# A two-pass channel-attention kernel: smaller last loads in pass one, and another order of the first stores in pass two

## The chip, the cores and the metric

The kernel runs on one core of a Trainium2 chip. The metric is the device time of one execution in microseconds (us). Three runs of the kernel before took 722.88, 720.63 and 720.82 us, so the median is 720.82 us.

## The reference

`x` has 384 x 384 pixels of 384 bf16 channels, 113 MB. Each channel is averaged over all pixels, the average is multiplied by one weight, goes through a sigmoid, and the result scales that channel everywhere:

```python
def reference(x, w1d):
    B, H, W, C = x.shape
    k = 1
    pad = k // 2
    g = jnp.einsum("bhwc->bc", x) / (H * W)
    gp = jnp.pad(g, ((0, 0), (pad, pad)))
    s = jnp.zeros_like(g)
    for i in range(k):
        s = s + gp[:, i:i + C] * w1d[i]
    s = _sigmoid(s)
    return x * s[:, None, None, :]
```

No output element can be written before the last input element has been read.

## The kernel before, in words

**Rows.** The 147,456 pixels lie on 128 partitions, so each partition owns 1152 pixels. A "row" below is one pixel on all 128 partitions: 128 x 384 bf16, 98,304 bytes in HBM and 768 bytes on each partition. The one big buffer, `arena`, holds 275 rows and cannot hold all 1152. So 367 rows are *kept* from pass one to pass two, and 785 rows are *streamed*: read in pass one for the sum alone and read again in pass two. In all 1152 + 785 rows are loaded and 1152 are stored, 3089 row transfers.

**Keeping more than fits.** Most kept rows are *folded* (`fold`, L292): four rows go into the space of three by moving the exponent bits of the fourth row (`u`) into bits of the other three that are the same for all plausible values. VectorE does this with bit operations (L276, L282), and ScalarE tests that no value was out of line (L313). Folding uses two scratch areas of eight rows, `T` (rows 259 to 266 of `arena`) and `Y` (rows 267 to 274). In pass two `unfold` (L470) takes the rows apart again and scales them. It writes into eight rows beside each group and uses `Y` as scratch. 71 kept rows are *raw*, not folded: `U` and `V` (8 rows each, beside the two columns of folded groups), the 39 rows of `A` (three slots of 13: `S1`, `S2`, `S3`), and at the very end the scratch areas themselves, `T` and `Y`, which lie next to each other and are filled once the last fold is done.

**Pass one.** Every load is issued from the SP queue (L236) and every row is summed over the partitions by a TensorE matmul against a matrix of ones, into one PSUM bank (L242). `take_raw` (L438) loads the raw rows and sums them. The loop at L437 does this, in program order, for `S2`, `U`, `S3`, `S1`, `V`, `Y`, and for `T` in two loads of 5 and 3 rows. Then ScalarE computes the sigmoid `s_bf` (L443) and puts a copy of it into PSUM (L447).

**Pass two** has a hand-written planner (L564 to L759), a Python loop that runs while the kernel is built. It keeps a model clock `now` that advances in steps of 0.05 us, and it decides in which order instructions are put on the queues. The names that matter here:

- `landed` is the queue of pieces in `arena` that wait to be scaled by VectorE (`scale`, L456). The loop at L620 fills it first, with `Y`, `U`, `T` and `V`. L622 adds the slots `S1` and `S2`. Three pieces of `S3` (4, 4 and 5 rows) are scaled by GpSimd instead, beside VectorE (`alongside`, L628).
- When a piece is scaled, `send` and then `store` (L466) put its store on the SP queue. In the planner's model a store occupies the DMA for `n * ROW + PER_STORE` us, with `ROW` 0.2267 and `PER_STORE` 0.061. It begins at the earliest `LAT` = 2 us after its issue, one transfer after the other, and is known to be over `SEEN` = 1.5 us after its end.
- `stored` (L609) then marks its rows `idle`, that is, free for a load. Rows of `Y`, `U` and `V` are not marked. They are what the unfolding of the two columns needs (`needed`, L607), and a column's first group starts only when its rows are stored.
- The load rule (L739 to L749) takes the longest run of idle rows. It issues a load of streamed rows if the run has at least 32 rows, or has 8 and the planned backlog of the DMA (`ahead`) is below `LOW` = 9 us, or if `ahead` is below `LAST` = 4 us.
- VectorE takes a landed piece if there is one, else the next step of an unfolding (L695 to L707).

**Queues.** All big transfers go through the one SP queue, in program order. A load into rows whose store is still under way makes SP wait until that store has landed, and everything behind it on SP waits too (L112, L118). Each SP transfer takes one of 24 semaphore lanes in turn, and also waits for the transfer 24 places before it (L46 to L52).

Of the kernel before, what the change touches and what calls it, by code (L numbers as in the profile page):

```python
# [127 lines left out]
def kernel(  # L128
# [28 lines left out]
    U = 3 * PIECE + PAIRS * 3 * PAIR  # L157
    G0 = U + PAIR
    V = G0 + PAIRS * 3 * PAIR
    A = V + PAIR  # L160
    N_A = 39
    T = A + N_A
    Y = T + 2 * PIECE
# [60 lines left out]
    def raw(a):  # L224

        return c_raw + (a - U if a < G0 else PAIR + a - V)
# [167 lines left out]
    S1, S2, S3 = ([slot] for slot in SLOTS)  # L394
# [38 lines left out]
    def take_raw(a, n):  # L433
        load(KEPT, a, raw(a), raw(a) + n)
        sum_rows(a, n)

    for a, n in S2 + [(U, 8)] + S3 + S1 + [(V, 8), (Y, 8), (T, 5), (T + 5, 3)]:  # L437
        take_raw(a, n)  # L438
    assert summed[0] == RPP

# [176 lines left out]
        return f  # L617


    for a, n, end in ((Y, 4, True), (Y + 4, 4, True), (U, 4, True), (U + 4, 4, True), (T, 8, True), (V, 8, True)):  # L620
        landed.append((KEPT, a, raw(a), n, end))
    for a, n in SLOTS[:2]:  # L622
        landed.append((KEPT, a, raw(a), n, True))
# [64 lines left out]
    while True:  # L688

        if dve_at <= now:  # L690
# [4 lines left out]
            if landed and (ahead < PENDING or not can):  # L695
                chunk, a, lo, n, end = landed.popleft()
# [13 lines left out]
        if alongside and alongside[0][0] <= now:  # L710
            _, chunk, a, lo, n = alongside.popleft()
            store(chunk, a, lo, lo + n)
            moves.append([now + LAT, n * ROW + PER_STORE, stored(a, n)])
        while waiting and waiting[0][0] <= now:
            _, n, then, chunk, a, lo, known = waiting.popleft()
# [12 lines left out]
        if bank_at is None and len(line) <= total - BANKS_AT and got and max(got)[0] >= PS * 4 // 3:  # L728
            a = max(got)[1]
# [9 lines left out]
        if got and todo < N_STREAM:  # L739
            n, a = max(got)  # L740
            n = min(n, CAP, N_STREAM - todo)
# [52 lines left out]
```

## Time and profile before

| what | us |
|---|---|
| median of the three runs | 720.82 |
| span of the profiled execution (first to last instruction) | 719.4 |
| first big load issued | 0.96 |
| sigmoid begins (L443) | 268.13 |
| first scale of pass two (L456) begins | 268.74 |
| first store issued on SP | 269.73 |
| first load of pass two issued on SP | 278.69 |
| VectorE busy in all | 493.9 |
| TensorE busy in all | 213.0 |

The profile gives no execution time of its own for the profiled execution beyond its span. The span of 719.4 us is 1.4 us below the median of the runs. An "issue" row on SP is the short time in which the sequencer hands a transfer over (0.33 us for most). The time "to landing" runs from that issue to the last of the transfer's 16 completion counts.

### The profile page before, as it was taken

To read this page: it belongs to the slowest core of one execution; us is meant where nothing else is said; L and a number is where in the kernel's file an instruction comes from. 1 tells how busy PE (TensorE), PEld (TensorE's weight loads), DVE (VectorE), ACT (ScalarE), POOL (GpSimd) and SP (SyncE) were. 2 spreads that over 40 slices of the span, in tenths; PEclk is the share of its full clock that TensorE was granted. 3 is DMA by queue.
4 is the path that set the end of the run, shared out by engine and by line. 5 is a ranking of instruction groups with operands and counts; after the bars stand their busy time and mean duration, and the time that the engine had idled before them with its cause. 6 is when DMAs were issued, how large, how long until landed. Compare 5 with 4: busy or idle time off the path is not lost.

```text
span 719.4 us, 2061 instructions
## 1 busy us (share of the span) xinstructions
PE 213.0 (30%) x1202; PEld 0.3 (0%) x3; DVE 493.9 (69%) x471; ACT 115.7 (16%) x93; POOL 10.6 (1%) x7
## 2 busy tenths in 40 slices
PE   4677788897987770000000000000000000000000
PEld 0000000000000000000000000000000000000000
DVE  4600004788999719988999998999998985095500
ACT  3600003566677610002000000000000000000000
POOL 0000000000000005000000000000000000000000
PEclk9899999999999995555555555555555555555555
DMA  9999999999999979999999999999999999999997
GB/s 379 435 433 435 426 428 435 438 434 425 426 426 429 427 326 376 421 391 423 430 430 437 430 428 441 428 433 435 430 436 433 429 437 428 441 432 427 440 439 314
DMA packets 20174, 303.79 MB, mean 422 GB/s; under 512 B 2243, under 2 KB 2243, under 8 KB 6083
## 3 DMA queue, kind: packets, MB, share of 16 engines
q1 hardware_dynamic: 20160, 303.67, 99.0%
q8 instruction: 4, 0.07, 0.0%
q14 instruction: 8, 0.06, 0.0%
q10 hardware_dynamic: 2, 0.00, 0.0%
HBM read 190.41 MB, written 113.25 MB: 422 GB/s over the span
## 4 chain that ended last, share of the span: by engine, by line
DMA 63%; DVE 23%; PE 6%; ACT 2%; another core or an unknown queue 1%; SPq 1%; issue 0%; DVEq 0%
DMA arena<-in_x_dram 42%; DMA out_dram<-arena 20%; DVE arena L456 16%; PE bank L242 6%; DVE arena L276 4%; DVE arena L282 3%; ACT arena L313 2%; SPq L236 1%; ACT s_bf L443 0%; SPq L789 0%; DVEq L112 0%; SPq L106 0%
## 5 line engine op out<-in xcount | busy, mean ns | idle before, releaser
L456 DVE TENSOR_TENSOR arena<-arena,s_bf 128x4608 bf16<-128x4608 bf16 (+8 forms) x97 | 228.7, 2390 | 68.2 <-DMA arena<-in_x_dram 52.2
L276 DVE TENSOR_SCALAR arena<-arena 128x1536 uint16<-128x1536 uint16 (+2 forms) x247 | 145.3, 633 | 111.6 <-DMA arena<-in_x_dram 101.8
L242 PE MATMUL bank<-arena,ones 128*128 128x384 bf16 x1151 | 204.6, 339 | 46.3 <-DMA arena<-in_x_dram 46.3
L313 ACT ACTIVATE arena<-arena 128x3072 uint16<-128x3072 uint16 (+1 forms) x38 | 102.4, 2696 | 142.1 <-DVE arena L276 142.1
L282 DVE TENSOR_TENSOR arena<-arena 128x1536 uint16<-128x1536 uint16 (+2 forms) x114 | 121.0, 1061 | 5.2 <-PE bank L242 2.8
L529 PE MATMUL bank<-odd,ones 128*128 128x1 bf16 x1 | 0.2, 187 | 322.6 <-DVE odd L524 322.6
L456 POOL TENSOR_TENSOR arena<-arena,s_bf 128x1536 bf16<-128x1536 bf16 (+1 forms) x3 | 10.4, 3481 | 268.7 <-ACT bank L447 268.7
L386 ACT COPY arena<-bank 128x512 uint32<-128x512 uint32 (+1 forms) x7 | 4.0, 570 | 58.2 <-DMA out_dram<-arena 58.1
L456 DVE TENSOR_TENSOR arena<-arena,bank 128x1536 bf16<-128x1536 bf16 (+2 forms) x7 | 11.3, 1689 | 0.0
L242 PE MATMUL bank<-zeros,ones 128*128 128x384 bf16 x48 | 8.3, 326 | 0.0
L313 ACT ACTIVATION_READ_ACCUMULATOR arena<-arena 128x1 f32 x38 | 7.1, 186 | 0.0
L386 ACT COPY bank<-arena 128x512 uint32<-128x512 uint32 (+1 forms) x7 | 3.6, 567 | 0.0
L443 ACT ACTIVATE s_bf<-bank,w_sc 128x384 bf16<-128x384 f32 x1 | 0.6, 580 | 14.5 <-PE bank L242 14.5
L256 PE MATMUL bank<-arena,ones 128*128 128x384 bf16 x1 | 0.5, 480 | 6.8 <-DMA arena<-in_x_dram 6.8
L762 ACT ACT_TABLE_LOAD x1 | 1.3, 1283 | 0.7 <-PEq L778 0.7
L343 DVE TENSOR_SCALAR w_sc<-bank 128x1 f32<-128x1 f32 x1 | 0.2, 157 | 1.2 <-PE bank L338 1.2
L333 DVE MEMSET ones<- 128x128 bf16 x1 | 0.2, 165 | 1.0 <-SPq L106 1.0
L338 PE MATMUL bank<-w_bf,ones 1*128 1x1 bf16 x1 | 0.2, 179 | 2.2 <-DMA w_bf<-in_w1d_dram 2.2
L529 PEld LDWEIGHTS bank<-odd,ones 128*128 128x128 bf16 x1 | 0.1, 105 | 581.5 <-DVE odd L524 581.5
L533 DVE CAST odd_i<-bank 128x1 int32<-128x1 f32 x1 | 0.2, 157 | 0.3 <-PE bank L529 0.3
L447 ACT COPY bank<-s_bf 128x192 uint32<-128x192 uint32 x1 | 0.3, 322 | 0.0
L519 DVE TENSOR_REDUCE worst<-seen 128x1 f32<-128x38 f32 x1 | 0.2, 186 | 0.0
(8 smaller groups left out, 0.9 us busy)
## 6 DMA issues: line engine op xcount, KB each, us to landing
arena<-in_x_dram SPq DMA_DIRECT2D x15, 4608.0 KB, 34.8
arena<-in_x_dram SPq DMA_DIRECT2D x21, 1248.0 KB, 13.5
out_dram<-arena SPq DMA_DIRECT2D x7, 3072.0 KB, 33.1
arena<-in_x_dram SPq DMA_DIRECT2D x6, 3072.0 KB, 27.5
out_dram<-arena SPq DMA_DIRECT2D x4, 4608.0 KB, 39.3
arena<-in_x_dram SPq DMA_DIRECT2D x6, 2304.0 KB, 18.5
arena<-in_x_dram SPq DMA_DIRECT2D x3, 4512.0 KB, 27.1
out_dram<-arena SPq DMA_DIRECT2D x10, 1248.0 KB, 11.9
```

What stands on the lines that cost most here:

```text
L236: lambda: nc.sync.dma_start(out=arena[:, a : a + hi - lo, :], in_=view(xf, r0, n)[:, lo:hi, :]),
L242: return pe.add_instruction(mybir.InstMatmult(name=nc.get_next_instruction_name(), ins=[pe.lower_ap(rhs), pe.lower_ap(ones[:])], outs=[pe. ...
L256: return nc.tensor.matmul(acc, lhsT=ones[:], rhs=arena[:, i, :], start=first, stop=last)
L276: lambda: nc.vector.tensor_scalar(out=dst, in0=src, scalar1=s0, scalar2=s1, op0=op0, op1=op1),
L282: "DVE", lambda: nc.vector.tensor_tensor(out=dst, in0=a, in1=b, op=op), reads=reads, writes=writes
L313: lambda: nc.scalar.activation(out=y, in_=y, func=ACTF.Copy, accum_out=seen[:, 2 * k + i : 2 * k + i + 1]),
L386: "ACT", lambda: nc.scalar.copy(dst.bitcast(u32), src.bitcast(u32)), reads=reads, writes=writes
L443: lambda: nc.scalar.activation(out=s_bf[:], in_=acc, func=ACTF.Sigmoid, scale=w_sc[:, 0:1]),
L447: "ACT", lambda: nc.scalar.copy(s_ps.bitcast(u32), s_bf[:].bitcast(u32)), reads=["s_bf"], writes=["bank0"]
L456: lambda: vec.tensor_tensor(out=v, in0=v, in1=s[:, None, :].to_broadcast([P, n, C]), op=Op.mult),
L529: lambda: nc.tensor.matmul(votes, lhsT=ones[:], rhs=odd[:], start=True, stop=True),
L762: nc.scalar.preload_act_table(ACTF.Sigmoid)
```

## The change

Two tuples of two loops are replaced. The first is the list of raw loads at the end of pass one. `Y` (8 rows) and `T` (5 + 3 rows) become five loads of 6, 4, 3, 2 and 1 rows, from the top of `Y` down to the first row of `T`. The second load (`T + 6`, 4 rows) covers the last two rows of `T` and the first two of `Y`. The second tuple is the order in which pass two scales and stores the first raw areas: `T` comes first, then `Y`, then `U`, which is now one piece of 8 rows, while `T` is two pieces of 4.

```diff
@@ -434,7 +434,7 @@
         load(KEPT, a, raw(a), raw(a) + n)
         sum_rows(a, n)
 
-    for a, n in S2 + [(U, 8)] + S3 + S1 + [(V, 8), (Y, 8), (T, 5), (T + 5, 3)]:
+    for a, n in S2 + [(U, 8)] + S3 + S1 + [(V, 8), (Y + 2, 6), (T + 6, 4), (T + 3, 3), (T + 1, 2), (T, 1)]:
         take_raw(a, n)
     assert summed[0] == RPP
 
@@ -617,7 +617,7 @@
         return f
 
 
-    for a, n, end in ((Y, 4, True), (Y + 4, 4, True), (U, 4, True), (U + 4, 4, True), (T, 8, True), (V, 8, True)):
+    for a, n, end in ((T, 4, True), (T + 4, 4, True), (Y, 4, True), (Y + 4, 4, True), (U, 8, True), (V, 8, True)):
         landed.append((KEPT, a, raw(a), n, end))
     for a, n in SLOTS[:2]:
         landed.append((KEPT, a, raw(a), n, True))
```

The planner itself is unchanged, but it runs on from the new order, so every later decision of pass two is taken anew.

## The prediction

> **What bounds the kernel now.** I read the page's 40 slices first, then the chain of waits, then the timeline around the pass boundary, then the windows, then single transfers.
>
> ```profile
> DMA  9999999999999979999999999999999999999997
> GB/s 379 435 433 435 426 428 435 438 434 425 426 426 429 427 326 376 421 391 423 430 430 437 430 428 441 428 433 435 430 436 433 429 437 428 441 432 427 440 439 314
> DMA packets 20174, 303.79 MB, mean 422 GB/s; under 512 B 2243, under 2 KB 2243, under 8 KB 6083
> DMA 63%; DVE 23%; PE 6%; ACT 2%; another core or an unknown queue 1%; SPq 1%; issue 0%; DVEq 0%
> ```
>
> The DMA is busy in every slice, and the chain that ended last is mostly DMA. 303.67 MB in 3089 row transfers at the usual 430 GB/s is 706 us of the 719.4 us span. The change moves no bytes away, so it can only win or lose what lies over that: slices 15, 16 and 18 (326, 376 and 391 GB/s), and the two ends. Slices 15 and 16 are the boundary:
>
> ```profile
> 261.59 3.57 PE L242 MATMUL bank<-arena,ones 128*128 128x384 bf16 x21 [0.68 <-DMA arena<-in_x_dram]
> 265.33 2.76 PE L242 MATMUL bank<-arena,ones 128*128 128x384 bf16 x16 [0.17 <-DMA arena<-in_x_dram]
> 268.13 0.58 ACT L443 ACTIVATE s_bf<-bank,w_sc 128x384 bf16<-128x384 f32 x1 [14.50 <-PE bank L242]
> 268.74 0.96 DVE L456 TENSOR_TENSOR arena<-arena,s_bf 128x1536 bf16<-128x1536 bf16 x1 [15.20 <-ACT s_bf L443]
> 269.73 8.91 SPq L466 DMA_DIRECT2D out_dram<-arena  x9
> ```
>
> The 21 matmuls are S1 and V. The 16 behind them are Y and both loads of T, and they run without a gap, so after 265.33 TensorE and not the DMA sets the end of pass one. Then come the sigmoid, the first scale and the first store. The stages by windows (length, then PE, PEld, DVE, ACT and POOL busy, granted clock, DMA share, GB/s):
>
> ```profile
> 265.00:267.00 2.00, 1.83 (x12) 0.00 (x0) 0.00 (x0) 0.00 (x0) 0.00 (x0) 1.00 0.35 139
> 267.00:270.50 3.50, 1.09 (x7) 0.00 (x0) 1.76 (x3) 0.90 (x2) 1.36 (x1) 1.00 0.00 0
> 270.50:280.00 9.50, 0.00 (x0) 0.00 (x0) 9.50 (x7) 0.00 (x0) 9.02 (x3) 0.60 1.02 418
> 280.00:285.00 5.00, 0.00 (x0) 0.00 (x0) 4.97 (x8) 0.00 (x0) 0.00 (x0) 0.50 1.02 334
> 285.00:310.00 25.00, 0.00 (x0) 0.00 (x0) 24.13 (x20) 0.00 (x0) 0.00 (x0) 0.50 1.01 421
> 310.00:315.00 5.00, 0.00 (x0) 0.00 (x0) 3.19 (x5) 0.00 (x0) 0.00 (x0) 0.50 1.00 320
> 420.00:700.00 280.00, 0.19 (x1) 0.10 (x1) 211.19 (x155) 0.00 (x0) 0.00 (x0) 0.50 1.01 434
> ```
>
> Nothing moves from 267.0 to 270.5. From 270.5 to 280 the DMA already runs at 418 GB/s, on stores alone. Two dips follow: 5 us at 334, worth 5 x (430 - 334) / 430 = **1.12 us**, and 5 us at 320, worth **1.28 us**. VectorE is full in 24.13 of 25 us between them, so there VectorE and the DMA bound together. The second dip has a visible cause on VectorE:
>
> ```profile
> 308.27 0.96 DVE L456 TENSOR_TENSOR arena<-arena,s_bf 128x1536 bf16<-128x1536 bf16 x1
> 311.81 1.16 DVE L456 TENSOR_TENSOR arena<-arena,s_bf 128x1920 bf16<-128x1920 bf16 x1 [2.58 <-DMA arena<-in_x_dram]
> ```
>
> VectorE ran out of landed rows for 2.58 us. On SP the load into slot S1 went out only at 310.50, when the slot's store, issued at 300.52 and 10.0 us under way, had landed. The few free slots go round too slowly there. The stalls of the first dip I can't name: the first load of pass two lies in it, but so do three stores.
>
> **Part one: the five last loads.** One row costs 0.227 us of DMA and 0.172 us of TensorE (2.76 / 16).
>
> ```profile
> arena<-in_x_dram SPq DMA_DIRECT2D x1, 768.0 KB, 11.3
> ...
> arena<-in_x_dram SPq DMA_DIRECT2D x1, 288.0 KB, 12.2
> ```
>
> The Y load was issued at 253.94 and landed 11.3 us later, at about 265.3. The 3-row load was issued at 254.89 and landed at 267.1. V (8 rows, issued 253.47, 9.9 us) landed at 263.4. The new loads follow V at 0.227 us a row, and I add 0.035 us a load (eight loads of 58 rows from 253.7 to 267.1 came 0.2 us later than their rows alone). They land at 264.8, 265.7, 266.4, 266.9 and 267.2. TensorE leaves V's rows at 265.16 and takes the 6, 4, 3, 2 and 1 rows at 0.172 us each, beginning at 265.16, 266.20, 266.89, 267.41 and 267.75, each after its landing. It ends at 267.93 instead of 268.09. The gain is the one idle gap, **0.16 us**, and no more, since TensorE is behind from 261.59 on: 37 rows at 0.172 us are 6.4 us however they are cut. The two added loads cost 0.07 us of DMA inside this cover; if TensorE had no backlog, they would delay the boundary by those 0.07 us. On SP they cost two issues of 0.48 us behind 254.89, with 10 us of transfers ahead of them: nothing. They shift the semaphore lanes by two; I count at most about nine transfers in flight, so the wait for the 24th before never holds.
>
> The Trainium skill's "DMA: Bandwidth & Descriptors", section Bandwidth, speaks against the cut: batch to at least 1 MiB for 75% of peak, smaller transfers are inefficient (it measured them one way, from GpSimd). By its 6.15 us for 1 MB, against 2.4 us of bytes at line rate, each load would bring some 3.7 us, an estimate from that page, and two more would cost over 7. The trace disagrees for queued transfers: the 288 KB load landed about 0.7 us behind the 480 KB one. No run here shows 1 or 2 rows.
>
> **Part two: the order of stores.** Scales are still four of 4 rows and two of 8; the seven that read the scale from PSUM stay seven. The stores stay six, and the first ends as early after the first scale. So the idle 267.0 to 270.5 is shortened by part one alone. What moves is the first load. I followed the planner's code by hand for the order alone. Before, T's store is the sixth on SP, with GpSimd's first between, and the first load stands behind S1's store. After, T's two stores come first, known as over at 5.4 and 6.4 on its clock. At 5.4 only 4 rows are idle and the backlog is 4.2 to 4.3, over `LAST` (4.0): no load. At 6.4 there are 8 and the backlog is about 5, under `LOW`: the load goes out behind U's store and ahead of V's. U's store takes the sixth place on SP, which was issued at 273.99, so the load is issued at about 274.2 instead of 278.69, 4.5 us earlier. T's second store has landed by then (the second store before was issued at 270.59, and the 384 KB stores take 2.5 us to land), so SP doesn't block.
>
> What it is worth: the DMA was full from 270.5 to 280 without it, so it fills no hole there; V's, GpSimd's second and S1's store move back by 8 rows, 1.8 us. T's rows are scaled a second time at about 284.6 (after the first unfolding step) instead of 289.2, and go round once more before 310. That is up to 16 row transfers, 3.6 us, more work for the DMA ahead of the second dip. Bounds on that dip: it closes (-1.28), or it stays (0), or it grows by the 8-row scale that is now ahead of the unfolding on a full VectorE (+1.7, from the 128x3072 scales of about 1.7 us). I take half, **-0.6**, since extra work is there but S1's slot, which SP waited for, comes round no earlier. The first dip goes wherever the first load goes: from -1.12 to +1.12, taken as 0. U is stored later and its group waits for it: landed by about 277.5, and unfolding starts near 280.7, so 3 us of cover. The replanning changes the number of later transfers by a few, at 0.035 us each: +/-0.2.
>
> **Sum:** -0.16 - 0.6 + 0 = -0.8 on a span of 719.4, so about 718.6 for the span, and with the 1.4 us between span and median **720.0 us**.
>
> **Rivals.** *Nothing to measure* (27%): the second dip stays since it hangs on S1; only -0.16, 720.7. For it: outside the dips the DMA moves 418 to 434 GB/s already. Against: the slots are tighter there than anywhere. The load not coming earlier at all, by the planner's guards, is in this case too; the backlog margins above speak against it. *Both dips go* (22%): -0.16 - 1.28 - 1.12 = -2.6, 718.2, and 717 if the engines also stay closer together at the end, where 700 to 717.6 moves only 355 GB/s (3.1 us lost). *Slower* (18%): the extra round of T on VectorE pushes the unfolding back, its 12-row and 4-row stores follow 1.7 us later, SP waits for them in order, and the slots behind come round later; once, +1.7 - 0.16 = 722.4, twice 724. It decides if VectorE is the tighter of the two bounds from 285 to 310; 24.13 of 25 us speak for it, the 421 GB/s of the same stretch against it. The forecast has 33%.
>
> **How the numbers follow.** This kernel can be told from no change at about 0.3%, 2.2 us: below 718.7 or above 723.0. Faster comes from most of the 22% and a little of the forecast's tail: 0.23. Slower from the upper half of the 18% and replanning accidents: 0.17. The rest, 0.60, is within. The range runs from 717.2 (both dips and some of the end) to 723.3 (one and a half rounds lost); the forecast's own is 719.2 to 720.7.
>
> **What would show it.** Part one: the last matmul of L242 at about 267.9, no idle gap over 0.1 us among the last 37, and the first scale at 268.6. Part two: the first load of pass two at about 274.2, seventh on SP. Second dip: GB/s from 310 to 315 above 320. Wrong, if TensorE waits among the last 16 rows, if VectorE's idle time near 310 grows, or if a new stretch under 400 GB/s appears after 330.

## The result, and the profile after

The changed kernel took 723.07 us (median of 20 runs) beside 721.93 us for the kernel before on the same chip (20 runs). The ratio is 1.0016, with a 95% interval of 1.0010 to 1.0023. It is slower, by 723.07 - 721.93 = 1.14 us. I had forecast 0.8 us faster. A change of this size is below the 0.3% that I had called the least that can be told; the 20 runs of each kernel resolve it.

The page of the changed kernel, with its span, the DMA rows of the 40 slices and the chain by engine:

```profile
span 720.6 us, 2059 instructions
...
DMA  9999999999999979999999999999999999999996
GB/s 382 429 441 428 426 432 432 434 435 430 425 426 428 428 317 391 425 430 414 388 430 438 431 425 437 428 440 436 430 429 442 429 436 435 431 432 433 427 440 298
...
DMA 69%; DVE 19%; PE 7%; ACT 1%; SPq 0%; issue 0%
```

The boundary still shows in slices 15 and 16. After it, slices 18 and 20 (430 and 388) stand where 391 and 430 stood: a slow place has gone, and a later one has come. The timeline around the boundary (start, length, engine, line):

```profile
261.68 6.17 PE L242 MATMUL bank<-arena,ones 128*128 128x384 bf16 x37 [0.68 <-DMA arena<-in_x_dram]
267.89 0.58 ACT L443 ACTIVATE s_bf<-bank,w_sc 128x384 bf16<-128x384 f32 x1 [14.16 <-PE bank L242]
268.51 0.96 DVE L456 TENSOR_TENSOR arena<-arena,s_bf 128x1536 bf16<-128x1536 bf16 x1 [14.87 <-ACT s_bf L443]
...
269.49 4.59 SPq L466 DMA_DIRECT2D out_dram<-arena  x6
274.18 0.40 SPq L236 DMA_DIRECT2D arena<-in_x_dram  x1
```

The 37 matmuls run without a gap, and the first scale begins 0.23 us earlier. The first load of pass two is seventh on SP and goes out 4.5 us earlier. The windows over the dips (last column GB/s; DVE busy is the third engine figure):

```profile
275.00:280.00 5.00, 0.00 (x0) 0.00 (x0) 5.00 (x3) 0.00 (x0) 4.28 (x2) 0.50 0.97 323
280.00:285.00 5.00, 0.00 (x0) 0.00 (x0) 4.97 (x8) 0.00 (x0) 0.00 (x0) 0.50 1.03 429
310.00:315.00 5.00, 0.00 (x0) 0.00 (x0) 4.96 (x6) 0.00 (x0) 0.00 (x0) 0.50 1.02 430
330.00:340.00 10.00, 0.00 (x0) 0.00 (x0) 9.26 (x5) 0.00 (x0) 0.00 (x0) 0.50 1.02 407
345.00:355.00 10.00, 0.00 (x0) 0.00 (x0) 9.35 (x11) 0.00 (x0) 0.00 (x0) 0.50 0.99 358
```

The last two of these stretches in the kernel before:

```profile
330.00:340.00 10.00, 0.00 (x0) 0.00 (x0) 7.62 (x8) 1.24 (x3) 0.00 (x0) 0.50 1.02 430
345.00:355.00 10.00, 0.00 (x0) 0.00 (x0) 9.97 (x10) 0.00 (x0) 0.00 (x0) 0.50 1.02 434
```

Against 430 GB/s, the first dip moved with the first load from 280-285 to 275-280 and kept its size: 5 x 107 / 430 = 1.24 us, where it was 1.12. The dip at 310 to 315 (1.28 us) is gone. Two new ones stand at 330 to 340 (10 x 23 / 430 = 0.53 us) and at 345 to 355 (10 x 72 / 430 = 1.67 us). Counted so, in one profile of each kernel, 1.28 us were won in one dip and 2.2 us lost in two later ones. This count leaves out the stretches between (see the open points below).

Where the two kernels begin to differ on VectorE is seen from 284 on. The kernel before:

```profile
284.61 1.35 DVE L276 TENSOR_SCALAR arena<-arena 128x4608 uint16<-128x4608 uint16 x1
285.87 0.95 DVE L282 TENSOR_TENSOR arena<-arena 128x1536 uint16<-128x1536 uint16 x1
286.74 4.22 DVE L456 TENSOR_TENSOR arena<-arena,s_bf 128x4608 bf16<-128x4608 bf16 x2
```

And the changed one:

```profile
284.37 1.75 DVE L456 TENSOR_TENSOR arena<-arena,s_bf 128x3072 bf16<-128x3072 bf16 x1
286.04 1.35 DVE L276 TENSOR_SCALAR arena<-arena 128x4608 uint16<-128x4608 uint16 x1
287.31 0.95 DVE L282 TENSOR_TENSOR arena<-arena 128x1536 uint16<-128x1536 uint16 x1
288.18 2.55 DVE L456 TENSOR_TENSOR arena<-arena,s_bf 128x4608 bf16<-128x4608 bf16 x1
```

In the first, the second unfolding step goes ahead and T's 8 rows are scaled behind it, inside the x2 group. In the second, T's 8 rows have come back earlier, are at hand when the first step ends, and are scaled 1.75 us ahead of the unfolding. The planner takes a landed piece first (L695) and goes on from there with another order. How late that makes the unfolding shows in the first load of 24 rows, which goes into rows that the unfolded groups have left. On SP, before and after:

```profile
355.99 5.15 SPq L236 DMA_DIRECT2D arena<-in_x_dram  x2
```

```profile
362.05 0.33 SPq L236 DMA_DIRECT2D arena<-in_x_dram  x1
```

Six microseconds later. Until then only four small slots go round. Not all of the six are delay: by the sizes of the issues in the traces, 415 rows of pass two stand ahead of this load on SP instead of 394, and the 21 rows more, all loads through the small slots, take 4.8 us at 0.227 us a row. So the time of this load tells which order a kernel runs, and only in small part how late it is.

What a deep dip after 300 is made of shows in the completion counts. In the kernel before, the 13-row load at 310.50 went out when the last count of its slot's store had come, at 310.48; the earliest of the 16 DMA engines had then 1.9 us of queued work left. In the changed kernel the 13-row load at 345.06 went out right behind the last count of a 13-row store, at 345.05, with 2.4 us left. On average over the 16 counts, each of the two loads landed 1.5 us further behind the transfer ahead of it than its rows take at 0.227 us each. The 8-row load at 333.71, behind a store that had landed at 333.69, lost 0.4 us in the same way. So a load waits for its slot, and meanwhile the queue runs down.

### The profile page after: what moved, and what is told of

Read it like the earlier page. It is cut to its first block, busy times and chain, and to the rows that moved or that the text cites. A ratio compares the mean times of both kernels' runs of the same rounds, so it can differ in the third digit from the quotient of the medians.

```text
span 720.6 us, 2059 instructions
## 1 busy us (share of the span) xinstructions
PE 210.4 (29%) x1202; PEld 0.3 (0%) x3; DVE 494.1 (69%) x471; ACT 115.7 (16%) x93; POOL 10.6 (1%) x7
## 4 chain that ended last, share of the span: by engine, by line
DMA 69%; DVE 19%; PE 7%; ACT 1%; SPq 0%; issue 0%
DMA arena<-in_x_dram 50%; DMA out_dram<-arena 18%; DVE arena L456 13%; PE bank L242 7%; DVE arena L276 4%; DVE arena L282 2%; ACT arena L313 1%; SPq L236 0%; ACT s_bf L443 0%; SPq L466 0%; SPq L789 0%; DVE worst L519 0%; SPq L106 0%
## 5 line engine op out<-in xcount | busy, mean ns | idle before, releaser
L242 PE MATMUL bank<-arena,ones 128*128 128x384 bf16 x1151 | 202.0, 336 | 48.7 <-DMA arena<-in_x_dram 48.6
L256 PE MATMUL bank<-arena,ones 128*128 128x384 bf16 x1 | 0.5, 479 | 6.8 <-DMA arena<-in_x_dram 6.8
```

Source lines behind the costliest of these rows:

```text
L242: return pe.add_instruction(mybir.InstMatmult(name=nc.get_next_instruction_name(), ins=[pe.lower_ap(rhs), pe.lower_ap(ones[:])], outs=[pe. ...
L256: return nc.tensor.matmul(acc, lhsT=ones[:], rhs=arena[:, i, :], start=first, stop=last)
```

## The experiments

Ratios are to the kernel before on the same chip, in five rounds, with the 95% interval.

**Each part alone.** The edits are the one changed line each.

```diff
-... + [(V, 8), (Y, 8), (T, 5), (T + 5, 3)]:
+... + [(V, 8), (Y + 2, 6), (T + 6, 4), (T + 3, 3), (T + 1, 2), (T, 1)]:
```

> The kernel before with the five last loads alone; pass two keeps its order. Theory A (the loss is all in the replanned slots of pass two): the last matmul about 0.2 us earlier, the time 0 to 0.2 us under before, ratio 0.9995 to 1.0003, dips of pass two where they were before (near 282 and 312). Theory B (the small loads themselves cost something): about as slow as the changed kernel, ratio 1.001 to 1.0023. Theory C (the loss is the lag of single DMA engines, which differs from execution to execution): no ratio over 1.0005, and a spread between the first and the last engine that differs from before's 3.0 us by up to 1 us either way without a cause in the order.

Measured: 0.9997 (0.9985 to 1.0008). The small loads cost nothing that can be seen, so theory B falls.

```diff
-    for a, n, end in ((Y, 4, True), (Y + 4, 4, True), (U, 4, True), (U + 4, 4, True), (T, 8, True), (V, 8, True)):
+    for a, n, end in ((T, 4, True), (T + 4, 4, True), (Y, 4, True), (Y + 4, 4, True), (U, 8, True), (V, 8, True)):
```

> The kernel before with the new order of stores alone; the last loads stay 8, 5 and 3. Theory A: ratio 1.0015 to 1.0025, with dips after 330 as in the changed kernel and none at 310 to 315. Theory B: ratio 0.9995 to 1.0005. Theory C: between, without new dips that recur at the same transfers.

Measured: 1.0024 (1.0013 to 1.0034), with 426 GB/s at 310 to 315, 376 at 330 to 340 and 349 at 345 to 355. The whole loss is in the order of the stores and in what the planner makes of it.

**The order without the early load.** One condition in the planner's load rule:

```diff
-        if got and todo < N_STREAM:
+        if got and todo < N_STREAM and now > 11.0:
```

> The changed kernel, but no load of pass two before the planner's clock is past 11.0, so that the first load goes out behind the store of slot S1 as before the change; the order of the first stores stays new. Theory A: the loss goes, ratio 0.9995 to 1.0003 as with the loads alone, and the dip near 312 is back. If the order of the first stores by itself costs (U's store late, its group held up), ratio 1.001 or more with the dips as before.

Measured: 0.9986 (0.9975 to 0.9997), a little better than expected. The dip at 310 to 315 is back (318 GB/s), and 330 to 340 and 345 to 355 are whole (429 and 432). The order of the first stores by itself costs nothing; the loss needs the first load ahead of S1's store.

**Is it the load's early place, or the order that follows?** The same condition with 9.0 and with 12.6. With 9.0 the load moves back two places and the later order stays that of the changed kernel. With 12.6 the later order is the old one.

> The changed kernel with the first load of pass two held only until the planner's clock is past 9.0: it goes out two places later, behind V's store and GpSimd's second one, and every transfer from S1's store on stands in the order of the changed kernel. Theory A (the loss is in the later order, where slots run short after 330): as slow as the changed kernel, ratio 1.001 to 1.0025, with the stretches 330 to 340 and 345 to 355 under 410 and 370 GB/s. Theory D (the load's early place itself costs, since it turns the DMA from stores to a load while the queue is shortest): half or more of the loss goes, ratio under 1.0008.

Measured: 1.0011 (1.0003 to 1.0020), with 382 GB/s at 330 to 340 and 372 at 345 to 355. This speaks for A, though the second stretch isn't under 370 and the interval doesn't shut out D's 1.0008.

> The same with the hold until 12.6: the load stands behind S1's store and GpSimd's last one, and from there the order is that of the kernel with the hold at 11.0. Theory A: the loss is gone, ratio 0.9980 to 1.0000, and no stretch under 400 GB/s after 330. Theory D: the ratio falls on evenly with the hold, and this is the fastest of the three holds.

Measured: 0.9993 (0.9984 to 1.0002), with 427 and 428 GB/s in the two stretches. D asked that it be the fastest of the three holds. It isn't, though its interval overlaps that of the hold at 11.0.

**Slots sooner, and the blocked load out of the way.** On SP the changed kernel shows this between 324 and 346:

```profile
324.53 9.52 SPq L236 DMA_DIRECT2D arena<-in_x_dram  x2
334.10 9.21 SPq L466 DMA_DIRECT2D out_dram<-arena  x3
345.06 0.34 SPq L236 DMA_DIRECT2D arena<-in_x_dram  x1
```

The second of the two loads went out at 333.71, when an 8-row store had landed. Behind it stood the store of a piece that VectorE had scaled by about 332:

```profile
329.23 5.42 DVE L456 TENSOR_TENSOR arena<-arena,s_bf 128x4992 bf16<-128x4992 bf16 x2
```

Two edits, each to the changed kernel:

```diff
-    BIG, CAP, PART, LOW, LAST = 32, 48, 16, 9.0, 4.0
+    BIG, CAP, PART, LOW, LAST = 32, 48, 16, 11.0, 4.0
```

> The changed kernel with the planner's LOW at 11.0 instead of 9.0: loads of 8 rows or more may go out while the planned backlog is still 11 us. The order is that of the changed kernel up to its first 24 transfers of pass two; after that slots are loaded about 2 us sooner. Theory A: the two slow stretches at 330 to 340 and 345 to 355 shrink to under half (above 415 and 400 GB/s) and the ratio falls to 0.9985 to 1.0005. If the loss is not in slots that come round too late, it stays at 1.001 to 1.0025.

Measured: 1.0017 (1.0003 to 1.0030), with 420 GB/s at 330 to 340 and 379 at 345 to 355. The first stretch is nearly whole, the second is not, and the time isn't better: a miss. By the expectation this speaks against slots that are loaded too late as such. A load still went out with a short queue, now at 342.32, when the earliest engine had 1.7 us left.

```diff
-        if got and todo < N_STREAM:
+        if got and todo < N_STREAM and not 64.9 < now < 68.2:
```

> The changed kernel with no load between 64.9 and 68.2 on the planner's clock: the 8-row load that held SP from 324.96 to 333.71 goes out behind the two 13-row stores that stood waiting behind it, and the plan runs on from there. Theory E (head-of-line blocking on SP makes the slow stretches): the stretch 330 to 340 is back above 420 GB/s and the ratio falls by 0.0005 to 0.0015, to 1.0000 to 1.001. Theory A alone (too few free rows, whatever stands first on SP): 330 to 340 stays under 415.

Measured: 1.0015 (1.0005 to 1.0025). 330 to 340 is whole (427 GB/s), but now 340 to 345 has 375 and 345 to 355 has 365. Taking the blocked load out of the way moved the dip and left the loss, so theory E explains the place of a dip. Theory A's own sign, 330 to 340 under 415, didn't come either: the shortage stayed, at another place.

**The one decision.** Both parts of the change, early load and all, with VectorE's choice at 284 turned back:

```diff
-            if landed and (ahead < PENDING or not can):
+            if landed and (ahead < PENDING or not can) and not 16.0 < now < 21.6:
```

> The changed kernel, both parts whole, with one decision of VectorE turned back: between 16.0 and 21.6 on the planner's clock no landed piece is scaled, so the second unfolding step of the first group goes ahead of the 8 rows that came back into T, as before the change. The first load of pass two still goes out ahead of V's store. From there every later transfer stands in the old order. Theory F (the loss comes from that one decision: T's extra round is put ahead of the unfolding, the group's rows come free later, and the slots run short after 330): the whole loss goes, ratio 0.9980 to 1.0002, the load of 24 rows back at about 356, no stretch under 400 GB/s after 330, and the stall with the first load still at 276 to 280. Theory D (the load's early place costs): ratio 1.0005 or more.

Measured: 0.9990 (0.9981 to 0.9999). Its windows, its VectorE from 284 on, and its load of 24 rows:

```profile
275.00:280.00 5.00, 0.00 (x0) 0.00 (x0) 5.00 (x3) 0.00 (x0) 4.58 (x2) 0.50 0.94 302
...
310.00:315.00 5.00, 0.00 (x0) 0.00 (x0) 3.49 (x6) 0.00 (x0) 0.00 (x0) 0.50 1.06 351
330.00:340.00 10.00, 0.00 (x0) 0.00 (x0) 7.38 (x7) 1.10 (x3) 0.00 (x0) 0.50 1.01 428
345.00:355.00 10.00, 0.00 (x0) 0.00 (x0) 9.97 (x10) 0.00 (x0) 0.00 (x0) 0.50 1.00 428
```

```profile
284.68 1.35 DVE L276 TENSOR_SCALAR arena<-arena 128x4608 uint16<-128x4608 uint16 x1
285.94 0.95 DVE L282 TENSOR_TENSOR arena<-arena 128x1536 uint16<-128x1536 uint16 x1
286.81 4.22 DVE L456 TENSOR_TENSOR arena<-arena,s_bf 128x4608 bf16<-128x4608 bf16 x2
```

```profile
355.84 5.16 SPq L236 DMA_DIRECT2D arena<-in_x_dram  x2
```

The first load still goes out early and its stall stands at 275 to 280. VectorE's rows are those of the kernel before, the 24 rows are back at 355.8, the two late dips and the loss are gone, and the dip at 310 to 315 has returned. On SP the transfers have the sizes of the kernel before, in its order, from the 11th of pass two on. Theory F holds for the decision: it picks the order that loses. It doesn't say which transfers of that order lose; the completion counts do, below. Theory D falls. The changed kernel beside it on the same chip:

> The changed kernel itself, unaltered, beside the others on one chip. Theories A and F: ratio 1.001 to 1.0025, the slow stretches at 330 to 340 and 345 to 355 again. Theory C (lag of single engines by chance): the spread between the first and the last engine at the end differs from the 3.8 us of the first profile by 0.5 us or more, and the loss with it.

Measured: 1.0018 (1.0009 to 1.0027), with both late dips at the same place:

```profile
330.00:340.00 10.00, 0.00 (x0) 0.00 (x0) 9.57 (x5) 0.06 (x1) 0.00 (x0) 0.50 1.01 365
345.00:355.00 10.00, 0.00 (x0) 0.00 (x0) 9.93 (x12) 0.00 (x0) 0.00 (x0) 0.50 0.99 352
```

Theory C's sign doesn't come: the last engine ended 3.5 us behind the first, 0.3 to 0.4 us less than in the first profile, and the loss is the same.

**A try to close the dip at 310 as well.** The kernel with the unfolding first, and smaller runs of free rows allowed, 4 in one and 5 in the other:

```diff
-            if n >= BIG or n == N_STREAM - todo or (ahead < LOW and n >= 8) or ahead < LAST:
+            if n >= BIG or n == N_STREAM - todo or (ahead < LOW and n >= 4) or ahead < LAST:
```

> The kernel with the unfolding first, and runs of 4 free rows instead of 8 are enough for a load when the planned backlog is under 9 us. In the plan no issue after the first 20 us finds a backlog under 7 us, where the old order has six such places about 310. If short slots make the dips: no stretch under 400 GB/s after 285, neither at 310 to 315 nor after 330, 1 to 2 us less against 0.3 us for nine more transfers: ratio 0.9965 to 0.9990. If the dips come from something else: 0.9985 to 1.0010.

Measured: 0.9996 (0.9987 to 1.0005). A miss: 310 to 315 is whole (424 GB/s), but 330 to 340 has 388, and the ratio lies where it was expected if the dips come from something else than short slots.

> The same with 5 rows. The plan keeps one place of short backlog (4.6 us, at 39.5 on its clock, about 308 us), for a shorter time. If short slots make the dips: 310 to 315 between 340 and 415 GB/s, ratio 0.9975 to 0.9998, between the two others.

Measured: 1.0038 (1.0025 to 1.0052), the slowest of all, with 327 GB/s at 310 to 315 and 391 at 315 to 330. A plain miss: a lower backlog in the plan doesn't say how deep the dip on the chip is.

**A load to warm the way.** A small extra load in the stretch without transfers, added to the kernel before:

```diff
+    fl.add(
+        "SP", lambda: nc.sync.dma_start(out=zeros[:, None, :], in_=view(xf, *STREAMED)[:, 0:1, 0:P]),
+        writes=["zeros"], dma=True, after=[fl.steps[-1]],
+    )
```

> The kernel before with one more small load, 256 bytes on each partition into a tile that is no longer used, issued after the last matmul of pass one, in the stretch in which no transfer runs. It adds nothing to what is computed. If the stall in and before the first load of pass two (about 1 us on the fastest engine, 2.6 us on the last one) is paid by the first read after a pause, it moves into that stretch and the time falls by 1 to 2.6 us, ratio 0.9965 to 0.9985. If it belongs to the turn from stores to a load in a short queue, it stays at 282 to 284 and the ratio is 0.9997 to 1.0005. Theory A says nothing of it; theory C: the lag of the last engine at the end changes with no relation to it.

Measured: 0.9992 (0.9982 to 1.0003), with 340 GB/s at 280 to 285. The stall stayed, so it isn't paid by a small read ahead of the stores. The extra load went out at 268.47 and the first big load at 279.04, with only stores between, so a price that comes back in 10 us without reads isn't shut out.

The kernels that keep the rule of 8 rows, by the issue of their first load of 24 rows:

| kernel | 24 rows at, us | GB/s 310-315 | 330-340 | 345-355 | ratio |
|---|---|---|---|---|---|
| load_held_126 | 355.2 | 360 | 427 | 428 | 0.9993 |
| loads_only | 355.3 | 366 | 428 | 431 | 0.9997 |
| unfold_first | 355.8 | 351 | 428 | 428 | 0.9990 |
| before | 356.0 | 320 | 430 | 434 | 1 |
| warm_load | 356.6 | 318 | 428 | 434 | 0.9992 |
| order_load_held | 356.8 | 318 | 429 | 432 | 0.9986 |
| after_low_11 | 359.9 | 425 | 420 | 379 | 1.0017 |
| after_swap | 360.5 | 427 | 427 | 365 | 1.0015 |
| after | 362.1 | 430 | 407 | 358 | 1.0016 |
| load_held_9 | 362.1 | 424 | 382 | 372 | 1.0011 |
| after_again | 363.2 | 427 | 365 | 352 | 1.0018 |
| order_only | 364.0 | 426 | 376 | 349 | 1.0024 |

Two groups, with nothing between them: the load of 24 rows goes out at 355 to 357 or at 360 to 364, and the ratio goes with it. But these are not twelve independent cases. From the 12th transfer of pass two on, the six kernels of the upper group have one order of transfers on SP, and four of the lower group another; only after_low_11 and after_swap have their own. The table shows that the ratio goes with the order, not that late 24 rows are the cost. The two kernels left out don't fit such a rule: with runs of 4 rows there is no load of 24 rows before 397 us and no loss, and with 5 it goes out at 360.3 in the slowest kernel of all.

What fits is the loads with a short queue. In all profiles of the table, the loads after 300 that went out with under 2.6 us of work left on the earliest engine are the ones at the dips. In the upper order there is one, near 310, and it lost 0.9 to 1.8 us on average over its 16 counts. In the lower order there are two, near 334 and 346, and they lost 1.9 to 2.8 us together. after_low_11 and after_swap have one each, at 342 to 343, with 1.6 and 2.1 us. The first of these lies inside the range of the upper order, so single profiles don't settle every case. Nor is a short queue a rule by itself: in the kernel with runs of 5 rows, a load at 344.89 with 2.2 us left lost 0.1 us.

The best versions, with both parts and either the load held or the unfolding first, are about 0.1% under the kernel before (0.9986 to 0.9993; the interval of the last reaches 1.0002). They cannot be told from each other.

## Why the prediction was wrong

- **The last loads.** Right, and a little larger than said: no gap in the last 37 matmuls, the first scale at 268.51 instead of 268.74 (0.23 us where I had 0.16), since the matmuls took 6.17 / 37 = 0.167 us each and not 0.172.
- **The first load.** Right: seventh on SP, at 274.18 (274.2 said), and it filled no hole. The first dip went with it at about its old size, as taken.
- **T's extra round.** Its place was right (284.37, 284.6 said), and so was the dip at 310 to 315, which closed altogether.
- **The step that failed** is the one that priced this round and what follows from it. I took -0.6 for the second dip and booked the round as up to 16 transfers won, and for everything later I had only a count: "The replanning changes the number of later transfers by a few, at 0.035 us each: +/-0.2." I followed the order up to the second dip and no further. The count was harmless, 89 transfers in pass two instead of 91, and the dip itself gave -1.28. But the rows to move are the same in number; what the round changed is which kind VectorE serves first. The 1.75 us scale ahead of the unfolding moved the planner onto another order, in which the small slots go round for 21 rows more and two loads go out with a short queue: 2.2 us by the windows between 330 and 355, a term that stood at nothing in my sum. It isn't a lasting delay of 1.7 us handed down: turning back the one choice brought the whole old order back.
- **The rival that came true** is the slower one, which named this mechanism: the extra round of T pushes the unfolding back and slots come round later. I gave it 18%. That its price of +1.5 us is near the 1.14 us measured is luck: it was one 1.7 us scale less 0.16, while in the measured loss one dip closed and two opened. What I held against it, 421 GB/s from 285 to 310, was read from the stretch before the loss. What I held for it, the full VectorE (24.13 of 25 us), may be the better witness, but that is argued only: no run made VectorE faster, and in the changed kernel it is busy for 22.99 us of that stretch.
- **Head-of-line waiting on SP**, which that rival had as well, set where the dip was; the loss stayed when one blocked load was taken out of the way (after_swap, 1.0015).

**Open.** How the loss splits in the first pair of profiles is not settled. The windows at the dips give the changed kernel about 0.9 us more in dips after 300 and 0.2 us less at the boundary, of 1.2 us more span, but these windows are picked. Over the whole stretch from 270.5 to 420 the two kernels moved 420 and 419 GB/s, 0.4 us apart. The 16 counts of the last store came 0.2 us later on average and 1.2 us later at the last of them, so most of the difference in this pair is the lag of single DMA engines: the last of the 16 ended 3.8 us behind the first, and 3.0 before. The pair from one chip, unfold_first and after_again, shows the loss without that lag: 419 and 414 GB/s over the same stretch, some 1.8 us, and 3.5 us between the first engine and the last in both. In single profiles of the upper group the lag was 2.4 to 3.9 us, in the lower 3.5 to 4.3. These overlap, so I can't say how much of the loss is chance in one profile. What makes the stall with the first load is also open.

## What to carry to other kernels

An earlier transfer on a full DMA won nothing in itself here (unfold_first with it, order_load_held without: 0.9990 and 0.9986); ask what it makes ready early, and what the next engine in line will then do first. Where that engine is full and some of its work frees large buffers, taking the small piece first can cost more, later, than the early load won. When a planner's order hangs on one comparison, follow the plan past the place that you hope to mend: the loss here lay 20 to 40 us behind it. Look there for loads that wait for their slot while little is queued ahead of them.

## What the runs showed of the hardware

A stall goes with the first load of pass two where that load has 8 rows. Against 430 GB/s over 5 us it is 1.0 to 1.5 us: 334 GB/s at 280 to 285 before, 340 there with the small load ahead of the stores, 323, 302 and 298 at 275 to 280 with the early load (after, unfold_first, order_only). With a first load of 4 rows (runs of 4 allowed) the stretch from 275 to 280 has 365 GB/s, 0.8 us.

Cutting the last loads to 2 rows and 1 row cost almost no rate: by the completion counts they landed 0.48 and 0.27 us behind the transfers before them, against 0.45 and 0.23 us for the rows alone. The rule of the Trainium skill's "DMA: Bandwidth & Descriptors", section Bandwidth, to batch to 1 MiB, isn't borne out for these loads of 96 and 192 KB, which waited in a full queue.

The 16 engines drift apart: the counts of one transfer lay within 0.2 us in the first stores of pass two and 2.4 to 4.3 us apart at its end. A slot is free only when the slowest engine has landed. At 345.06 in the changed kernel the counts of the store that the load waited for lay between 341.24 and 345.05, and the earliest engine was through with all that was queued at 347.50; its next count, of a load that takes 2.95 us at 0.227 us a row, came 4.3 us later.
